# One transposition type and one matmul shape in a fused long-convolution and gated-MLP kernel

## The chip, the core and the metric

The kernel runs on one core of a Trainium2 chip. The metric is the device time of one execution in microseconds (us). Before the change it is 233.99 us, the median of three runs (233.98 to 234.03). In what follows PE is TensorE, PEld its weight loads, DVE VectorE, ACT ScalarE, POOL GpSimd, and SP the engine whose queue issues nearly all DMAs.

## What is computed

The input x has 2048 rows of 640 elements; xn is its layer norm. The output is x plus two branches of xn.

```python
k_shift = sum over t of k_pad[:, t:t + S, :] * shift_k[:, ks - 1 - t]   # 4 taps
kv  = k_shift * v
y   = irfft(rfft(kv_pad) * rfft(kf_pad))[:S]       # long convolution, length 2048, per channel, with ssm_k
y   = y + kv * ssm_D
A   = q * y                                        # q = xn
B   = (sigmoid(xn @ w_gate) * (xn @ w_up)) @ w_down    # 640 -> 1728 -> 640
out = x + A + B
```

The kernel adds ssm_D to the first sample of the filter h (ssm_k), so that the term kv * ssm_D comes out of the convolution itself.

## The kernel before

**Branch B** goes over the rows in four rounds t of 512. For each of 13 blocks fc of 128 hidden features there is a gate product (`gate_mm`, five matmuls of 512 columns), a sigmoid on ACT (`gate_ev`), an up product (`up_mm`, five more) and a multiplication on DVE that writes hT (`up_ev`, L286). A fourteenth half block has its own functions. Then `down_mm` (L315) turns hT into the output rows and `down_ev` (L320, DVE) adds them to x. The products, the down products and the last stage of the convolution all take their PSUM tiles from one ring of four banks, psG. A tile of that ring can be written again only when its reader is through: for an up product that is `up_ev`, for a down product `down_ev`, both on DVE.

**Branch A** goes over the 640 channels in five chunks c of 128. A chunk's time samples are held as (p, b): time = 16 p + b, with p on the 128 partitions and b in 0 to 15. One tile per chunk, kvh, has shape [128, 2, 16, 128]: plane 0 is kv, plane 1 is the filter h; there are two such tiles in turn.

- `kv_op` (L348 to L357, 16 DVE instructions a chunk) makes kv in plane 0, in two halves of eight b.
- h comes from DRAM as [channel, time] into the tile hn and has to be turned so that time lies on partitions. `h_turn(c, n)` (L334) does that on DVE with the engine's 32 x 32 block transposition, two instructions a chunk, each for half of the b. It reads hn as 4-byte elements, that is pairs of neighbouring samples, so each instruction moves 512 elements a partition, and the result holds the two samples of a pair next to each other: h of sample b = 2 b' + e and channel c lies at (b', c, e).
- `add_D` (L328, POOL) adds ssm_D to one row of the turned h.
- `st1_mm(c, n)` is the first stage of the transform. For each of four b it multiplies the table S1 (128 x 128 weights) with kv's 128 columns (L374) and with h's 128 columns (L376), which it reads with a step of two elements. Both results go side by side into one PSUM tile of the ring psC (two tiles), which `st1_ev` copies out, mostly on ACT. The eight calls of a chunk hold 64 matmuls, 320 in all.
- Further stages follow: a trip through DRAM, `st2_mm` (L418), the product of the two spectra on DVE (`prod`, L431 and L433), the inverse `inv1_mm` (L447), another trip through DRAM, `inv2_mm` (L488), and `inv2_q` and `inv2_x` on DVE, which multiply by xn and add to x.

**The order** of all this is written out by hand: each engine's instructions are issued in the order of one string of letters (`ORDER`), H being `h_turn`, a `st1_mm`, k one instruction of `kv_op`, u the DVE side of branch B, g the PE side. An engine takes its instructions strictly in that order, so an instruction that takes longer delays everything behind it on that engine.

Of the kernel before, what the change touches and what calls it, by code (L numbers as in the profile page):

```python
# [11 lines left out]
F32 = mybir.dt.float32  # L12
# [7 lines left out]
P = 128  # L20
NB = S // P
# [36 lines left out]
def kernel(  # L58
# [14 lines left out]
    nc = tc.nc  # L73
# [27 lines left out]
    S1 = S1t.bitcast(BF16)  # L101
# [23 lines left out]
    cin = [dict() for _ in range(NC)]  # L125
# [36 lines left out]
    def slot(c):  # L162

        if "kvh" not in cin[c]:
            cin[c]["kvh"] = cv.tile([P, 2, NB, P], BF16, name="kvh", bufs=2)
        return cin[c]["kvh"]
# [157 lines left out]


    def add_D(c):
        h0 = cin[c]["kvh"][0:1, 1, 0:2, :].rearrange("p b c -> p (b c)").rearrange("p (c e) -> p e c", e=2)[:, 0, :]
        nc.gpsimd.tensor_tensor(h0, h0, cin[c]["dr"][:, :], ALU.add)  # L328

    def h_turn(c, n):  # L330

        hv = cin[c]["hn"].bitcast(F32).rearrange("p k (r b) -> p b k r", b=8)
        to = slot(c)[:, 1, :, :].rearrange("p b c -> p (b c)").bitcast(F32).rearrange("p (b k r) -> p b k r", b=8, k=4)
        nc.vector.transpose(to[:, 4 * n:4 * n + 4, :, :], hv[:, 4 * n:4 * n + 4, :, :])  # L334

    def kv_op(c, n):

# [28 lines left out]
    def st1_mm(c, n):  # L366

        h, n4 = divmod(n, 4)
        if n == 0:
            chunks[c]["d1"] = dr.tile([P, 2, NB, 2 * P], BF16, name="d1", bufs=2)  # L370
        pss[n] = ps = psC.tile([P, 4, 2 * P], F32, name="ps1", tag="c")
        for i in range(4):
            b = 4 * n4 + i
            nc.tensor.matmul(ps[:, i, 0:P], lhsT=S1[:, b, h, :], rhs=cin[c]["kvh"][:, 0, b, :], start=True, stop=True)  # L374
            hp = cin[c]["kvh"][:, 1, :, :].rearrange("p b c -> p (b c)").rearrange("p (b c e) -> p b e c", b=8, e=2)
            nc.tensor.matmul(ps[:, i, P:2 * P], lhsT=S1[:, b, h, :], rhs=hp[:, b // 2, b % 2, :], start=True, stop=True)  # L376

    def st1_ev(c, n, copy=act_copy):
        d = chunks[c]
# [222 lines left out]
    for c in range(NC):  # L602
        for n in range(2):
            step("H", h_turn, c, n)
        step("D", add_D, c)
        for n in range(8):
            step("a", st1_mm, c, n)
            step("A", st1_ev, c, n)
# [101 lines left out]
```

## Time and profile before

| what | value |
|---|---|
| median of three runs | 233.99 us |
| span of the profiled execution, first to last instruction | 232.4 us |
| what lies around the span (median minus span) | 1.6 us |
| PEld busy | 130.7 us, 2201 loads |
| ACT busy | 123.0 us, 154 instructions |
| POOL busy | 13.3 us, 26 instructions |
| h_turn starts, ten instructions | from 30.9 us to 120.4 us |
| st1_mm starts | from 41.4 us to 162.8 us |
| granted PE clock, mean over the span | 1.000 |

The page of a profile gives busy times; matmuls are pipelined, so the busy time of a group of them (its instructions' union) is more than what it adds to the chain. What a matmul adds is the distance between the starts of neighbours. In the trace, L374 is followed by L376 after 55.2 ns in the mean (160 pairs), L376 by the next L374 after 58.5 ns (129 pairs without other work between); a matmul of 320 columns by its like after 136 ns, one of 512 columns after 216 ns.

### The profile page before, as it was taken

The numbers are of one execution on the slowest core, as the hardware profiler recorded it, in microseconds if no ns is written. First come the engines' busy times: TensorE is split into PE (matmuls) and PEld (weight loads), VectorE is DVE, ScalarE is ACT, GpSimd is POOL, SyncE is SP. The second block draws the span as 40 slices with busy tenths as digits, with TensorE's granted clock in tenths as the row PEclk, the third lists the DMA queues.
The fourth block names the chain that finished last, engine by engine and source line by source line (L and its number), as shares of the span: only waits on it lengthen the run. The fifth ranks groups of instructions, "written<-read, shape, count | busy, mean of one in ns | idle before, by whom it ended". The sixth has DMA issues, their size and how long they took to land.

```text
span 232.4 us, 5436 instructions
## 1 busy us (share of the span) xinstructions
PE 227.3 (98%) x2201; PEld 130.7 (56%) x2201; DVE 203.9 (88%) x362; ACT 123.0 (53%) x154; POOL 13.3 (6%) x26
## 2 busy tenths in 40 slices
PE   7999999999999999999999999999999999999995
PEld 2754445877454556667554544478654544446772
DVE  5534799999989999999999999997799999997773
ACT  2433232595354877766775847673555667752000
POOL 5210010040001100000010300000000000000000
PEclk9999999999999999999999999999999999999999
DMA  6999999799999979999989999597989998364784
GB/s 179 320 328 238 265 312 293 201 249 148 336 209 322 290 263 241 273 210 237 331 236 268 272 258 300 171 218 203 260 247 276 290 257 246 119 170 115 224 265 136
DMA packets 96303, 56.79 MB, mean 244 GB/s; under 512 B 55894, under 2 KB 90518, under 8 KB 96022
## 3 DMA queue, kind: packets, MB, share of 16 engines
q1 hardware_dynamic: 95846, 56.12, 90.6%
q8 instruction: 17, 0.28, 0.5%
q10 hardware_dynamic: 432, 0.33, 0.5%
q14 instruction: 8, 0.07, 0.1%
HBM read 36.12 MB, written 18.35 MB: 234 GB/s over the span
## 4 chain that ended last, share of the span: by engine, by line
PE 95%; DVE 2%; DMA 1%; ACT 0%; issue 0%
PE pd L315 27%; PE pu L271 24%; PE pg L271 24%; PE psb L488 4%; PE ps L376 4%; PE ps L374 4%; PE ps L418 3%; PE psa L447 2%; PE pg L292 2%; DVE st L198 1%; DMA x<-in_A_q_dram 1%; PE pu L262 1%; PE pg L262 1%; PE pt L244 0%; DVE xn L219 0%; ACT xnT L247 0%
## 5 line engine op out<-in xcount | busy, mean ns | idle before, releaser
L271 PEld LDWEIGHTS <-w 128*128 128x128 bf16 x500 | 46.6, 98 | 54.2 <-issue 4.7
L315 PE MATMUL pd<-wd,hT 128*128 128x320 bf16 (+2 forms) x448 | 66.0, 299 | 0.0
L271 PE MATMUL pg<-xnT,w 128*128 128x512 bf16 x250 | 62.2, 379 | 0.1
L271 PE MATMUL pu<-xnT,w 128*128 128x512 bf16 x250 | 62.2, 379 | 0.0
L315 PEld LDWEIGHTS <-hT 128*128 128x128 bf16 x448 | 41.7, 98 | 18.2 <-issue 2.4
L280 ACT ACTIVATE sig<-pg 128x512 bf16<-128x512 f32 x52 | 31.1, 601 | 31.1 <-PE pg L271 27.3
L286 DVE TENSOR_TENSOR hT<-sig,pu 128x512 bf16<-128x512 bf16 x52 | 34.9, 680 | 11.6 <-PE pu L271 7.5
L234 ACT CAST xz<-ps 128x1024 bf16<-128x1024 f32 x36 | 35.1, 1014 | 15.8 <-PE ps L418 15.7
L234 ACT CAST t<-ps 128x1024 bf16<-128x1024 f32 x24 | 23.7, 1013 | 16.3 <-PE ps L376 14.1
L433 DVE TENSOR_TENSOR xz<-xz 128x2048 bf16<-128x2048 bf16 x20 | 24.4, 1219 | 0.2
L376 PE MATMUL ps<-kvh,S1t 128*128 128x128 bf16 x160 | 21.4, 219 | 0.0
L374 PE MATMUL ps<-kvh,S1t 128*128 128x128 bf16 x160 | 21.4, 217 | 0.0
L354 DVE TENSOR_TENSOR acc<-acc,tmp 128x1024 bf16<-128x1024 bf16 x30 | 20.4, 681 | 0.3
L352 DVE TENSOR_TENSOR tmp<-kx,sc 128x1024 bf16<-128x1024 bf16 x30 | 20.4, 680 | 0.3
L320 DVE TENSOR_TENSOR x<-pd,x 128x320 bf16<-128x320 f32 (+2 forms) x32 | 15.2, 482 | 3.8 <-PE pd L315 3.6
L374 PEld LDWEIGHTS <-S1t 128*128 128x128 bf16 x160 | 15.5, 97 | 2.5
L376 PEld LDWEIGHTS <-S1t 128*128 128x128 bf16 x160 | 15.4, 96 | 2.5
L234 ACT CAST TBt<-ps 128x1024 bf16<-128x1024 f32 x14 | 13.8, 1012 | 4.0 <-PE ps L376 3.9
L198 DVE BATCH_NORM_STATS2 st<-x 128x6 f32<-128x320 bf16 x32 | 13.9, 475 | 1.9 <-DMA x<-in_A_q_dram 1.9
L493 DVE TENSOR_TENSOR yx<-psb,xn 128x512 bf16<-128x512 f32 x20 | 13.7, 686 | 1.4 <-PE psb L488 0.8
L431 DVE STREAM_SHUFFLE xz<-xz 128x512 f32<-128x512 f32 x20 | 14.6, 728 | 0.0
L234 ACT CAST ao<-psa 128x1024 bf16<-128x1024 f32 x9 | 9.0, 1013 | 8.3 <-PE psa L447 6.9
(55 smaller groups left out, 159.8 us busy)
## 6 DMA issues: line engine op xcount, KB each, us to landing
t<-d SPq DMA_DIRECT2D x15, 512.0 KB, 6.0
d<-t SPq DMA_DIRECT2D x13, 512.0 KB, 4.9
d<-TBt SPq DMA_DIRECT2D x7, 512.0 KB, 5.8
d<-ao SPq DMA_DIRECT2D x6, 512.0 KB, 5.5
bi<-d SPq DMA_DIRECT2D x6, 512.0 KB, 5.3
kx<-in_A_k_dram SPq DMA_DIRECT2D x10, 256.0 KB, 5.9
hn<-in_A_ssm_k_dram SPq DMA_DIRECT2D x20, 128.0 KB, 5.0
kvh<-in_A_v_dram SPq DMA_DIRECT2D x10, 256.0 KB, 5.2
```

Source lines behind the costliest of these rows:

```text
L198: nc.vector.bn_stats(d["st"][:, i, s2, :], x[:, b, s2 * 320:(s2 + 1) * 320])
L234: nc.scalar.copy(out=out, in_=in_)
L271: nc.tensor.matmul(pg[:, :], lhsT=w[:, c, u * UP + fc * P:u * UP + (fc + 1) * P], rhs=xnT[:, :, c, :], start=(c == 0), stop=(c == NC - 1))
L280: nc.scalar.activation(sig[fc][:, :], pgs[0, fc][:, :], ACT.Sigmoid)
L286: nc.vector.tensor_tensor(hT[:, fc, :], sig[fc][:, :], pgs[1, fc][:, :], ALU.mult)
L315: nc.tensor.matmul(pd[:, :], lhsT=hT[:, fc, bb * P:(bb + 1) * P], rhs=wd[:, fc, es], start=(fc == 0), stop=(fc == NFC - 1))
L320: nc.vector.tensor_tensor(x[:, 4 * t + bb, es], pds[bb, half][:, :], x[:, 4 * t + bb, es], ALU.add)
L352: nc.vector.tensor_tensor(d["tmp"][:, :, :], kx[:, lo + 3 - m:hi + 3 - m, :], sb(m), ALU.mult)
L354: nc.vector.tensor_tensor(d["acc"][:, :, :], d["acc"][:, :, :], d["tmp"][:, :, :], ALU.add)
L374: nc.tensor.matmul(ps[:, i, 0:P], lhsT=S1[:, b, h, :], rhs=cin[c]["kvh"][:, 0, b, :], start=True, stop=True)
L376: nc.tensor.matmul(ps[:, i, P:2 * P], lhsT=S1[:, b, h, :], rhs=hp[:, b // 2, b % 2, :], start=True, stop=True)
L433: nc.vector.tensor_tensor(z[:, 1:3, :, :], z[:, 0:1, :, :].to_broadcast((P, 2, 8, P)), z[:, 1:3, :, :], ALU.mult)
```

## The change

The diff has two parts. `h_turn` reads hn as 2-byte elements and writes plane 1 in the same layout as plane 0, (b, channel); each of the ten instructions now moves 1024 elements a partition where it moved 512 of twice the size, and the bytes are the same. `add_D` follows the new layout. In `st1_mm` the two matmuls of 128 columns with the same weights become one of 256 columns that takes both planes, so that there are 160 in place of 320. The order string is the same.

```diff
     def add_D(c):
-        h0 = cin[c]["kvh"][0:1, 1, 0:2, :].rearrange("p b c -> p (b c)").rearrange("p (c e) -> p e c", e=2)[:, 0, :]
+        h0 = cin[c]["kvh"][0:1, 1, 0, :]
         nc.gpsimd.tensor_tensor(h0, h0, cin[c]["dr"][:, :], ALU.add)

     def h_turn(c, n):

-        hv = cin[c]["hn"].bitcast(F32).rearrange("p k (r b) -> p b k r", b=8)
-        to = slot(c)[:, 1, :, :].rearrange("p b c -> p (b c)").bitcast(F32).rearrange("p (b k r) -> p b k r", b=8, k=4)
-        nc.vector.transpose(to[:, 4 * n:4 * n + 4, :, :], hv[:, 4 * n:4 * n + 4, :, :])
+        hv = cin[c]["hn"].rearrange("p k (r b) -> p b k r", b=NB)
+        to = slot(c)[:, 1, :, :].rearrange("p b (k r) -> p b k r", k=4)
+        nc.vector.transpose(to[:, 8 * n:8 * n + 8, :, :], hv[:, 8 * n:8 * n + 8, :, :])
...
             b = 4 * n4 + i
-            nc.tensor.matmul(ps[:, i, 0:P], lhsT=S1[:, b, h, :], rhs=cin[c]["kvh"][:, 0, b, :], start=True, stop=True)
-            hp = cin[c]["kvh"][:, 1, :, :].rearrange("p b c -> p (b c)").rearrange("p (b c e) -> p b e c", b=8, e=2)
-            nc.tensor.matmul(ps[:, i, P:2 * P], lhsT=S1[:, b, h, :], rhs=hp[:, b // 2, b % 2, :], start=True, stop=True)
+            nc.tensor.matmul(ps[:, i, :], lhsT=S1[:, b, h, :], rhs=cin[c]["kvh"][:, :, b, :], start=True, stop=True)
```

## The prediction

> **What bounds the kernel now.** I read the page first: the busy times, the slices, and the chain that ended last.
>
> ```profile
> PE 227.3 (98%) x2201; PEld 130.7 (56%) x2201; DVE 203.9 (88%) x362; ACT 123.0 (53%) x154; POOL 13.3 (6%) x26
> ...
> DVE  5534799999989999999999999997799999997773
> ...
> PEclk9999999999999999999999999999999999999999
> ...
> PE 95%; DVE 2%; DMA 1%; ACT 0%; issue 0%
> ```
>
> PE carries the chain. But DVE is at 9 tenths in nearly every slice from the seventh on, so the second view is the window in which the ten transpositions and nearly all of the first stage lie.
>
> ```profile
> 30.30:158.40 128.10, 128.02 (x1199) 74.97 (x1197) 124.15 (x221) 80.68 (x99) 7.99 (x10) 1.00 0.96 255
> ```
>
> After the stretch and its length come PE, PEld, DVE, ACT and POOL busy. PE is busy for 128.0 of 128.1 us and DVE for 124.2 (the rest is mostly gaps of some 0.03 us between dependent instructions). Two engines are full at once; the chain names one. What tells whether DVE has room is its own timeline: in this stretch it waits over 0.2 us for others three times, the last at the very end.
>
> ```profile
> 65.18 0.69 DVE L286 TENSOR_TENSOR hT<-sig,pu 128x512 bf16<-128x512 bf16 x1 [0.46 <-ACT sig L280]
> 68.83 0.69 DVE L286 TENSOR_TENSOR hT<-sig,pu 128x512 bf16<-128x512 bf16 x1 [0.26 <-ACT sig L280]
> 158.43 1.23 DVE L237 CAST t<-ps 128x1024 bf16<-128x1024 f32 x1 [1.22 <-PE ps L376]
> ```
>
> The fourth view is the groups of instructions:
>
> ```profile
> L376 PE MATMUL ps<-kvh,S1t 128*128 128x128 bf16 x160 | 21.4, 219 | 0.0
> L374 PE MATMUL ps<-kvh,S1t 128*128 128x128 bf16 x160 | 21.4, 217 | 0.0
> L354 DVE TENSOR_TENSOR acc<-acc,tmp 128x1024 bf16<-128x1024 bf16 x30 | 20.4, 681 | 0.3
> L431 DVE STREAM_SHUFFLE xz<-xz 128x512 f32<-128x512 f32 x20 | 14.6, 728 | 0.0
> L334 DVE STREAM_TRANSPOSE kvh<-hn 128x512 f32<-128x512 f32 x10 | 10.9, 1098 | 0.0
> ```
>
> A transposition takes 1098 ns for 512 elements, a shuffle of 512 contiguous elements of the same size 728.
>
> **PE's part.** A pair L374, L376 now takes 55.2 + 58.5 = 113.7 ns from start to start. Between 320 columns (136 ns) and 512 (216 ns) a column costs 80 / 192 = 0.417 ns; 256 columns come to 136 - 64 x 0.417 = 109.3. So 160 pairs save 160 x 4.4 = 0.7 us, 0.14 us a chunk. Bounds: the jump between the two planes could cost what the step of two costs now, 3.3 ns (saving 0.2 us), or nothing. The 160 weight loads that fall away lay beside matmuls (PEld 56% busy): nothing. `add_D` (POOL, 0.4 to 0.8 us, 6% busy) is the same instruction on contiguous elements: nothing.
>
> **DVE's part.** No 2-byte transposition stands in this trace. From below: 2-byte multiplications such as L354 move 1024 elements in the time in which L286 moves 512 with one 4-byte operand (start to start of the next independent instruction 0.60 us each); if a transposition did that it would drop from 1.03 to about 0.6 us, 0.43 less. From above: twice the whole instruction, 1.03 us more. I take the row itself: same engine, same instruction, the same step of 32 bytes between the elements read (8 of 4 bytes before, 16 of 2 bytes after). It takes 1.027 us from its start to the next one's in the mean of the nine that stand alone or end a pair. About 0.08 of that is fixed: measured the same way, L433 takes 1.13 for 2048 elements and L352 0.60 for 1024, which leaves 0.07; the copy L237 takes 1.13 for 1024 and the shuffle 0.62 for 512, which leaves 0.11. So an element costs 0.947 / 512 = 1.85 ns, against 0.54 / 512 = 1.05 in the shuffle. I hold that this is the price of an element that is fetched alone, and that it does not halve with the element's size. Then a new instruction takes 1024 x 1.85 + 80 = 1.97 us, 0.95 more; ten of them 9.5 us. Within this theory the added 512 elements cost at least the shuffle's rate, 0.54 us, and at most 1.03.
>
> [...]
>
> **From DVE's delay to the end.** DVE issues in order, so each transposition delays all behind it. I follow DVE's lag D against the old times and ask at each place where PE needs DVE how far ahead DVE was (the slack: PE's old start minus DVE's old end). The tightest are in the ring psG, where an up product needs the bank that `up_ev` of two blocks before frees. The last of them that counts:
>
> ```profile
> 121.44 0.63 DVE L286 TENSOR_TENSOR hT<-sig,pu 128x512 bf16<-128x512 bf16 x1
> ...
> 122.45 0.59 PE L271 MATMUL pu<-xnT,w 128*128 128x512 bf16 x2
> ```
>
> DVE ends at 122.07, PE starts at 122.45: slack 0.38.
>
> - Two transpositions from 30.9: D = 1.9. The up product at 35.41 had no slack (`up_ev` ended at 35.57 by the records): PE is 1.9 late.
> - Third, 42.3: D = 2.85. At 54.50 the first stage starts 0.07 after kv of chunk 1 is done: PE 2.8 late.
> - Fourth, 55.7: D = 3.8; slack 0.48 at 63.39: PE 3.3 late. DVE's waits of 0.46 and 0.26 take D down to PE's 3.3.
> - Fifth and sixth, 71.6 and 81.9: D = 5.2; slack 0.36 at 89.99: PE 4.9 late.
> - Seventh and eighth, 95.2: D = 7.1; slack 0.82 at 116.78: 6.3.
> - Ninth and tenth, 118.8: D = 9.0; slack 0.38 at 122.45: **PE 8.6 late**.
>
> Behind this PE is full and nothing gives the time back: DVE's later waits (1.22 us at 158.43 and others) are waits for PE, which is late itself. PE's own saving mostly goes under, since PE waits for DVE until 122; only the pairs after it count, 32 of chunk 4, 0.14 us. The sum is +8.6 - 0.1 = +8.5 us. The span goes from 232.4 to 240.9, and with the 1.6 us around it the median from 234.0 to **242.5 us**. In general the sum is ten times the added price less about 1.0: 0.54 gives 238.4, 1.03 gives 243.3. If DVE had had cover for the lag (it has none before 158), only the part over it would show.
>
> SP's queue waits behind hn's loads for `h_turn` (the load of the next chunk needs hn free), and wr1, rd2 and the rest stand behind them. That delay is D, and PE is late by nearly as much, so I add nothing; if a transfer becomes the last to arrive it is by D - PE's delay, under 0.9 us, in the middle, and the next step of D covers it. Bound 0 to 0.9.
>
> **Rivals.**
>
> 1. *The transposition goes by bytes* (place: L334; price: none; it decides if 2-byte elements take half a 4-byte element's time). [...] Against it: nothing in the 1.85 ns hints at bytes, and the shuffle, which moves 4 bytes an element, costs 1.05. Then DVE stays as it is and PE may gain only what the slacks allow: 0.38 at 122.45, then 0.14 on chunk 4: 234.0 - 0.5 = 233.5 us. Not slower.
> 2. *One element a cycle, hops or none.* Priced at the shuffle's 1.05 ns, 1024 elements and 0.08 come to 1.15 us, 0.12 more; by the same walk D is 1.2 less 0.2 for the waits, PE 0.6 late, 234.6 us. Against it: the 4-byte instruction doesn't run at that rate. [...]
> 3. *Two elements a cycle*, 0.6 us: DVE gains room, PE keeps all of its 0.7 us: 233.3. Nothing but L354 speaks for it.
> 4. *DVE's lag is partly covered*, because PE's order lets slack grow that I don't see: some 4 us in place of 8.5, 238. Against it: slacks under 0.5 us at 35.4, 54.5, 63.4, 90.0 and 122.5.
> [...]
>
> **Chances.** Forecast 0.80; rivals 0.05, 0.05, 0.03, 0.04, 0.03. The range reaches from the lower price of the theory, 238.4, with rival 4 nearly in it, to its upper price with the queue's 0.9: 243.3 + 0.9 = 244.2, rounded to 244.4. What lies outside is rivals 1, 2, 3 and 5, 0.16, and a little of the forecast's own tails. A measurement of this kernel can tell 0.2%, 0.5 us, from no change. Faster by more: rival 3 and half of rival 1, 0.06. Within: half of rival 1 and half of rival 2, 0.05. Slower: 0.89.
>
> **What would show it.** Price: L334 at about 2.0 us (start to next start), ten times. Path: DVE at 98% or more between 30 and 165, and PE with about 8.5 us of idle time, named as waits for DVE's hT, kvh or x (L286, L357, L320) or for ACT's sig behind them; the chain of waits should move from PE to DVE in this stretch. PE's part: one L374 group of 160, 109 ns apart. The forecast is wrong if L334 stays near 1.1 us, or if it doubles and PE still shows no idle time.

## The result and the profile after

The changed kernel takes 242.44 us (median of six runs, 242.32 to 244.08) against 234.07 (233.98 to 234.36) for the kernel before on the same chip. The ratio is 1.037, with a 95% interval of 1.0343 to 1.0397. The profiled execution has a span of 240.6 us where it had 232.4.

The page of the changed kernel: busy times, DVE's slices, and the chain that ended last.

```profile
PE 227.9 (95%) x2041; PEld 127.9 (53%) x2041; DVE 212.8 (88%) x362; ACT 123.2 (51%) x154; POOL 13.3 (6%) x26
...
DVE  5544899999999999999999999997889999898673
...
PE 62%; DVE 27%; issue 6%; DMA 3%; ACT 1%; SPq 0%; DVEq 0%
```

PE has 160 instructions less and about the same busy time, DVE has 8.9 us more in the same 362 instructions. The chain, which was PE's to 95%, now runs over DVE for 27% of the span. DVE's share of the span is 88% as before: the span grew with it, so the share shows nothing. The stretch that ran from 30.3 to 158.4 us now ends at about 167:

```profile
30.30:167.00 136.70, 129.36 (x1056) 72.87 (x1055) 133.38 (x222) 80.93 (x99) 7.97 (x10) 1.00 0.92 238
```

After the stretch and its length, PE's busy time comes first, DVE's third. Before, both filled 128.1 us (128.0 and 124.2); now DVE fills 133.4 of 136.7 and PE leaves 7.3 idle. The groups that the change touches (busy time, mean ns of one, idle time before them and what ended it):

```profile
L374 PE MATMUL ps<-kvh,S1t 128*128 128x256 bf16 x160 | 22.7, 273 | 2.5 <-DVE kvh L357 2.5
...
L334 DVE STREAM_TRANSPOSE kvh<-hn 128x1024 bf16<-128x1024 bf16 x10 | 20.2, 2024 | 0.0
```

A transposition went from 1098 to 2024 ns; from its start to the next instruction's, which is what DVE loses, from 1.025 to 1.947 us (mean of ten each; the prediction has 1.027). The 273 ns of a matmul are no cost, since matmuls overlap: a merged one starts 109.3 ns after the one before (mean of 128 places without other work between). Where PE waits is seen in its timeline: these six rows are all its waits over 0.1 us behind 30 us, with what ended each in brackets.

```profile
37.50 1.24 PE L292 MATMUL pg<-xnT,w 128*128 128x512 bf16 x5 [0.82 <-DVE hT L286]
...
57.38 0.60 PE L374 MATMUL ps<-kvh,S1t 128*128 128x256 bf16 x4 [1.74 <-DVE kvh L357]
...
66.11 0.61 PE L374 MATMUL ps<-kvh,S1t 128*128 128x256 bf16 x4 [0.40 <-DVE kvh L357]
...
91.63 0.61 PE L374 MATMUL ps<-kvh,S1t 128*128 128x256 bf16 x4 [0.40 <-DVE kvh L357]
...
116.68 0.43 PE L416 MATMUL ps<-t,SMt 32*32 32x512 bf16 x14 [1.72 <-DVE t L237]
...
130.77 1.24 PE L271 MATMUL pu<-xnT,w 128*128 128x512 bf16 x5 [2.16 <-DVE hT L286]
```

All six end with DVE, and none comes after 131 us; before the change there was none. Five of them wait for what the prediction's walk follows, hT or kv; the one at 116.68 waits for a tile of the ring psC, which DVE's copy L237 has to read first. They add up to 7.2 us. A wait is counted from the modelled end of the matmul ahead, which lies some 0.16 us behind the time at which the next could have started (a product of 512 columns lasts 379 ns and its like follows after 216), so six waits stand for about 8.2 us. That is the difference of the spans. Matched instruction by instruction with the kernel before, PE is 0.03 us late at 33 us, 1.1 at 41, 2.9 at 54.5, 3.2 at 63, 3.6 at 90, 6.0 at 117, 8.3 at 122.5 (old times), and 8.2 at the end.

### The profile page after: what moved, and what is told of

Same layout as the page of the kernel before. It is cut to its first block, busy times and chain, and to the rows that moved or that the text cites. A ratio compares the mean times of both kernels' runs of the same rounds, so it can differ in the third digit from the quotient of the medians.

```text
span 240.6 us, 5118 instructions
## 1 busy us (share of the span) xinstructions
PE 227.9 (95%) x2041; PEld 127.9 (53%) x2041; DVE 212.8 (88%) x362; ACT 123.2 (51%) x154; POOL 13.3 (6%) x26
## 4 chain that ended last, share of the span: by engine, by line
PE 62%; DVE 27%; issue 6%; DMA 3%; ACT 1%; SPq 0%; DVEq 0%
PE pd L315 16%; PE pu L271 16%; PE pg L271 15%; DVE acc L354 5%; DVE kvh L334 5%; PE psb L486 4%; DVE tmp L352 4%; DVE st L198 3%; PE ps L374 3%; PE ps L416 3%; PE psa L445 2%; DVE hT L286 2%; DVE x L320 2%; DMA kx<-in_A_k_dram 2%; DVE kvh L357 2%
## 5 line engine op out<-in xcount | busy, mean ns | idle before, releaser
L271 PEld LDWEIGHTS <-w 128*128 128x128 bf16 x500 | 47.3, 98 | 56.8 <-issue 6.9
L315 PEld LDWEIGHTS <-hT 128*128 128x128 bf16 x448 | 42.2, 98 | 18.9 <-issue 2.6
L374 PE MATMUL ps<-kvh,S1t 128*128 128x256 bf16 x160 | 22.7, 273 | 2.5 <-DVE kvh L357 2.5
L354 DVE TENSOR_TENSOR acc<-acc,tmp 128x1024 bf16<-128x1024 bf16 x30 | 20.4, 682 | 0.3
L374 PEld LDWEIGHTS <-S1t 128*128 128x128 bf16 x160 | 15.3, 98 | 9.7 <-DVE kvh L357 2.1
L334 DVE STREAM_TRANSPOSE kvh<-hn 128x1024 bf16<-128x1024 bf16 x10 | 20.2, 2024 | 0.0
L486 PEld LDWEIGHTS <-TBt 128*128 128x128 bf16 x160 | 10.0, 98 | 3.5 <-issue 1.8
## 6 DMA issues: line engine op xcount, KB each, us to landing
hn<-in_A_ssm_k_dram SPq DMA_DIRECT2D x20, 128.0 KB, 3.7
```

The source lines that it names most:

```text
L271: nc.tensor.matmul(pg[:, :], lhsT=w[:, c, u * UP + fc * P:u * UP + (fc + 1) * P], rhs=xnT[:, :, c, :], start=(c == 0), stop=(c == NC - 1))
L315: nc.tensor.matmul(pd[:, :], lhsT=hT[:, fc, bb * P:(bb + 1) * P], rhs=wd[:, fc, es], start=(fc == 0), stop=(fc == NFC - 1))
L334: nc.vector.transpose(to[:, 8 * n:8 * n + 8, :, :], hv[:, 8 * n:8 * n + 8, :, :])
L354: nc.vector.tensor_tensor(d["acc"][:, :, :], d["acc"][:, :, :], d["tmp"][:, :, :], ALU.add)
L374: nc.tensor.matmul(ps[:, i, :], lhsT=S1[:, b, h, :], rhs=cin[c]["kvh"][:, :, b, :], start=True, stop=True)
```

## The experiments

The kernels below ran on chips on which single executions spread more than in the comparison above: the kernel before took 234.4 to 234.5 us in the median, with 233.9 to 236.7 in all. So 0.4 us of a time that was expected against 234.0 is the chip's. Differences under about 0.5 us are therefore read from the traces, not from the medians.

### Is it the transposition or the matmul?

First each part of the change by itself. The transposition alone (an edit of the changed kernel):

```diff
-            nc.tensor.matmul(ps[:, i, :], lhsT=S1[:, b, h, :], rhs=cin[c]["kvh"][:, :, b, :], start=True, stop=True)
+            for s in range(2):
+                nc.tensor.matmul(ps[:, i, s * P:(s + 1) * P], lhsT=S1[:, b, h, :], rhs=cin[c]["kvh"][:, s, b, :], start=True, stop=True)
```

> The transposition alone: 2-byte elements and the new layout, but the first stage keeps two matmuls of 128 columns for each b (both on contiguous columns). Theory (DVE's price sets the end; PE's saving counts only behind the last place where PE waits for DVE): L334 at 1.95 us from start to start as in the changed kernel, the time within 0.3 us of the changed kernel's 242.4, that is 242.3 to 242.7. Rival (the merged matmul itself delays something): under 241.5. Rival (the merged matmul saves its full 0.7 us in the changed kernel): 243.1.

Measured: 242.64 us (242.38 to 242.87), ratio to the kernel before 1.034 (1.0293 to 1.0381). The transposition alone has the whole cost, and each instruction its new length:

```profile
L334 DVE STREAM_TRANSPOSE kvh<-hn 128x1024 bf16<-128x1024 bf16 x10 | 20.2, 2027 | 0.0
```

Its two contiguous matmuls of 128 columns start 56 ns apart, 112 ns a pair, so the pair of the old kernel (113.7) lost 1.7 ns to h's step of two elements, and the merge itself is worth 2.7 ns more.

The merge alone, on the kernel before:

```diff
-            nc.tensor.matmul(ps[:, i, 0:P], lhsT=S1[:, b, h, :], rhs=cin[c]["kvh"][:, 0, b, :], start=True, stop=True)
-            hp = cin[c]["kvh"][:, 1, :, :].rearrange("p b c -> p (b c)").rearrange("p (b c e) -> p b e c", b=8, e=2)
-            nc.tensor.matmul(ps[:, i, P:2 * P], lhsT=S1[:, b, h, :], rhs=hp[:, b // 2, b % 2, :], start=True, stop=True)
+            nc.tensor.matmul(ps[:, i, :], lhsT=S1[:, b, h, :], rhs=cin[c]["kvh"][:, :, b, :], start=True, stop=True)
```

> The matmul of 256 columns alone: the transposition stays at 4-byte elements, so that h's columns of two neighbouring samples are mixed in what is multiplied, and the output is not the reference's. Theory: one matmul each 109 ns in place of a pair in 113.7, but PE may run ahead of DVE only by the slacks: 234.0 - 0.5 = 233.5, and no longer than 234.1. Rival (matmul of two runs of 128 columns costs more than the pair): over 234.3. Rival (PE alone sets the time): the full 0.7 less, 233.3.

Measured: ratio 1.0023 (0.9992 to 1.0053), lowest run 233.52 against 233.87 before. The interval holds no change and the expected 0.5 us less is just outside it; the run excludes that the merge costs what the change costs, and can't settle its sign. One more kernel asked for that: the merge together with a cheaper transposition (contiguous reading, next section), so that DVE has room.

> The merged matmul with the 4-byte transposition read contiguously (0.63 us in place of 1.03, as measured in the contiguous run): what the merge is worth when DVE has room. Two samples of h are mixed in what is multiplied and samples land in wrong places, so the output is not the reference's. Theory (PE's saving is lost only because PE waits for DVE): the 0.7 us appear, 0.7 us under the kernel before (0.5 to 0.8). Rival (the merge saves nothing on PE, whatever DVE does): within 0.2 us of the kernel before.

Measured: ratio 1.0018 (0.9996 to 1.004), lowest 233.59 against 233.94 before. By the time the expected gain did not appear. The trace of one run, matched with the kernel before, shows where it went in that run: PE starts 0.62 us late (at 7 us, ahead of any changed instruction, behind x's first loads), loses 0.63 at 54.5, since DVE had waited 0.9 us for x, and 0.1 at 58 behind a DMA of xnT. From there its lag only shrinks, from 1.24 us to 0.76, by about 0.018 with every call of `st1_mm`; with the 0.12 of the first chunk that makes 0.6 of the 0.7 us. In the 2-byte run of the next section, where DVE has room too, PE's lag shrinks in the same way, by 0.34 us between 58 and 122. So the traces have the saving on PE, and landings of DMAs outweigh it in this one. That they do so in the median of all runs is not shown, and neither is a gain in time.

### Why does a 2-byte transposition cost twice?

The forecast rested on a price, 1.85 ns, for an element that is read with a step of 32 bytes. The test changes only the order in which hn is read:

```diff
-        hv = cin[c]["hn"].rearrange("p k (r b) -> p b k r", b=NB)
+        hv = cin[c]["hn"].rearrange("p k (b r) -> p b k r", b=NB)
```

> The changed kernel with one thing altered: the transposition reads hn in contiguous order (32 neighbouring samples a block) in place of every sixteenth sample. The bytes, the count of elements and all other work are the same; the samples of h land in the wrong places, so the output is not the reference's. Theory (1.85 ns is the price of an element fetched alone with a step of 32 bytes): L334 falls to about 1.15 us from start to start (1024 x 1.05 + 80 ns), and the time to 234.6 (234.1 to 235.2). Rival (the transposition takes near two cycles an element however it reads): L334 stays at 1.95 us and the time at 242.4.

The same in the kernel before, on 4-byte elements:

> The kernel before with the transposition of 4-byte elements reading contiguously, output not the reference's for the same reason. Theory: L334 falls from 1.03 to 0.62 us from start to start, ten times 0.41 off DVE; PE has no idle time to give, so the time stays within 0.2 us of 234.0. Rival (two cycles an element however it reads): L334 at 1.03 and 234.0.

The transposition's group in the first and in the second of these runs:

```profile
L334 DVE STREAM_TRANSPOSE kvh<-hn 128x1024 bf16<-128x1024 bf16 x10 | 12.2, 1231 | 0.0
```

```profile
L334 DVE STREAM_TRANSPOSE kvh<-hn 128x512 f32<-128x512 f32 x10 | 6.9, 699 | 0.0
```

2024 became 1231 ns and 1098 became 699; to the next start 1.16 and 0.62 us. The 512 elements between the two contiguous runs cost 532 ns, 1.04 each. The 2-byte run took 235.47 us (234.91 to 236.31), ratio 1.0036 (1.0011 to 1.0062), so 7 us of the change's cost went away with the order of reading alone, at the same number of elements and bytes. In the trace PE ends 0.7 us late, 0.2 of it from ahead of the first transposition. The expected 234.6 is 1.0026 times 234.0 and lies within the interval; the 235.47 itself lies above the expected 235.2, as this chip's kernel before lies above 234.0. The 4-byte run took 234.34, ratio 0.9992 (0.9968 to 1.0015): ten times 0.4 us off DVE bought nothing, as PE had no idle time to give.

How far apart must elements lie? One kernel gave each chunk another step, on 2-byte elements, and one on 4-byte elements. The edit of the first (the second reads 4-byte elements with steps of 8, 4, 2, 1 and 16 elements):

```diff
-        hv = cin[c]["hn"].rearrange("p k (r b) -> p b k r", b=NB)
-        to = slot(c)[:, 1, :, :].rearrange("p b (k r) -> p b k r", k=4)
-        nc.vector.transpose(to[:, 8 * n:8 * n + 8, :, :], hv[:, 8 * n:8 * n + 8, :, :])
+        step = (16, 8, 4, 2, 1)[c]
+        flat = cin[c]["hn"].rearrange("p k t -> p (k t)")[:, 1024 * n:1024 * n + 1024]
+        hv = flat.rearrange("p (a r b) -> p a b r", b=step, r=32)
+        to = slot(c)[:, 1, 8 * n:8 * n + 8, :].rearrange("p b c -> p (b c)").rearrange("p (a b r) -> p a b r", b=step, r=32)
+        nc.vector.transpose(to, hv)
```

> The price of the step, 2-byte elements: the changed kernel, with the transposition of chunk 0, 1, 2, 3, 4 reading every 16th, 8th, 4th, 2nd element and each element (steps of 32, 16, 8, 4 and 2 bytes), 1024 elements each time; h's samples land in wrong places, so the output is not the reference's. Theory (an element that is fetched alone costs 1.85 ns, neighbours 1.04): chunk 0 at 2.0 us an instruction, chunk 4 at 1.23, and the time between 234.6 and 242.4. [...] Rival (the price grows with the step): five different durations.

> The same with 4-byte elements: the kernel before, with chunk 0, 1, 2, 3, 4 reading with steps of 32, 16, 8, 4 and 64 bytes, 512 elements each time; the output is not the reference's for the same reason. [...] The time stays within 0.5 us of the kernel before.

DVE's timeline in the first, one row for the steps of 32, 16, 8 and 2 bytes (start, length):

```profile
31.01 2.03 DVE L336 STREAM_TRANSPOSE kvh<-hn 128x1024 bf16<-128x1024 bf16 x1
...
44.30 2.02 DVE L336 STREAM_TRANSPOSE kvh<-hn 128x1024 bf16<-128x1024 bf16 x1
...
74.85 1.24 DVE L336 STREAM_TRANSPOSE kvh<-hn 128x1024 bf16<-128x1024 bf16 x1
...
122.54 1.24 DVE L336 STREAM_TRANSPOSE kvh<-hn 128x1024 bf16<-128x1024 bf16 x1
```

And in the second, for 32, 16, 8 and 64 bytes:

```profile
30.93 1.10 DVE L337 STREAM_TRANSPOSE kvh<-hn 128x512 f32<-128x512 f32 x1
...
57.70 1.09 DVE L337 STREAM_TRANSPOSE kvh<-hn 128x512 f32<-128x512 f32 x1
...
73.34 0.70 DVE L337 STREAM_TRANSPOSE kvh<-hn 128x512 f32<-128x512 f32 x1
...
120.42 1.05 DVE L337 STREAM_TRANSPOSE kvh<-hn 128x512 f32<-128x512 f32 x1
```

There are two prices and no steady slope: steps of 2, 4 and 8 bytes cost 1.24 us for 1024 elements, steps of 16 and 32 cost 2.0; with 4-byte elements 0.70 for 512 at 4 and 8 bytes, 1.1 at 16 and 32, and a little less, 1.05, at 64. In both runs the edge lies between the steps of 8 and 16 bytes. The times, one run each, are 237.7 and 235.96 us beside 235.17 for the kernel before on that chip. The second is 0.8 us over, where at most 0.5 was expected; in its trace DVE waits 1.28 us for hn and 0.42 for x ahead of 46 us, and PE is 1.7 us late from 57 us to the end, so its time says nothing about the price. The durations of the transpositions do.

### Does the lag add up as the walk said?

The change in the last two chunks only, and in the first three only (`c >= 3` or `c <= 2` selects old or new code in `add_D`, `h_turn` and `st1_mm`):

> A partial dose: chunks 0 to 2 as before the change, chunks 3 and 4 as after it (four of the ten transpositions in 2-byte elements, at 95 and 119 us, and their first stage merged). Theory (lag adds up and is passed to PE at the next place without slack): D = 4 x 0.92 = 3.7 by 121, slack 0.4 at 122.45, 0.1 saved on PE: 234.0 + 3.2 = 237.2 (236.7 to 237.8). Rival (the early chunks, where PE has least slack, make the cost, the late ones are covered): under 235.5. Rival (a share of the whole, 4 / 10 of 8.4): 237.4, which this run can't tell from the theory; the first three chunks alone can.

> The other part of the dose: chunks 0 to 2 as after the change, 3 and 4 as before it. Theory: D = 6 x 0.92 - 0.5 (DVE's two waits) = 5.0 by 83, and nothing is added later, so that the places with slack 0.8 at 116.8 and 0.4 at 122.45 decide: 234.0 + 5.0 - 0.4 - 0.1 = 238.5 (238.0 to 239.1). The two partial doses then add up to some 0.7 less than the whole, since each has the slack once. Rival (share of the whole, 6 / 10 of 8.4): 239.0. Rival (the late chunks make the cost): under 236.5.

Measured: 237.94 us (237.67 to 240.23), ratio 1.0159 (1.011 to 1.0207), and 239.46 (238.83 to 240.92), ratio 1.0208 (1.0156 to 1.026). Both lie above the middle of what was expected, by 0.7 and 1.0 us, and just outside the expected ranges, which ended at 237.8 and 239.1; 0.4 us of each is the chip's. Early and late chunks both count: the rival of the covered late chunks is out, and so is the one of the covered early ones. The rival of plain shares (237.4 and 239.0) is not: with the chip's 0.4 us it fits these times better than the theory, and the two doses together cost no less than the whole, where 0.7 us less was expected.

The traces, matched with the kernel before at its own times, split the excess. In the late dose PE is 0.5 us late at 59, before any changed instruction (DVE had waited 0.52 us for x), and 3.8 to 3.9 us late behind 122: 3.3 from the dose, where 3.2 was expected. In the early dose PE is 0.64 late from the start, and DVE's lag is 5.6 us from 83 to 127. PE is 5.25 late behind 122, so 4.6 came from DVE, where 4.5 was expected. It is 5.7 late from 143 on, and that last step is no wait for DVE: the product of the last convolution stage at 149.11 in this run (143.41 before) waits 0.28 us for the DMA that reads bi, which SP issued at 142.07 where it had issued it at 134.61. So the queue's term, bounded by 0 to 0.9 us in the prediction, is real: 0.4 us where no later lag of DVE covers it. The walk along DVE is good to 0.1 us in these two runs; landings of DMAs, which are not in its sum, make the rest.

### Two tries at a version that beats both

If DVE gets a contiguous transposition of 4-byte elements and PE the merged matmul, both gain. That needs another pair: two channels in place of two samples, laid side by side and sorted by sample ahead of the transposition. POOL was to do it (an edit of the changed kernel):

```diff
     def h_turn(c, n):

-        hv = cin[c]["hn"].rearrange("p k (r b) -> p b k r", b=NB)
-        to = slot(c)[:, 1, :, :].rearrange("p b (k r) -> p b k r", k=4)
-        nc.vector.transpose(to[:, 8 * n:8 * n + 8, :, :], hv[:, 8 * n:8 * n + 8, :, :])
+        h1 = slot(c)[:, 1, :, :]
+        pairs = h1.rearrange("p b (k r e) -> p b k r e", k=2, e=2)
+        bs = slice(8 * n, 8 * n + 8)
+        for kk in range(2):
+            src = cin[c]["hn"][:, 2 * kk:2 * kk + 2, :].rearrange("p e (r b) -> p b r e", b=NB)
+            nc.gpsimd.tensor_copy(pairs[:, bs, kk, :, :], src[:, bs, :, :])
+        hv = h1.rearrange("p b c -> p (b c)").bitcast(F32).rearrange("p (b k r) -> p b k r", b=NB, k=2)
+        nc.vector.transpose(hv[:, bs, :, :], hv[:, bs, :, :])
```

The loads of hn (in `load_h`, not shown) change with it.

> A version that keeps the merged matmul and gives DVE a cheaper transposition than before the change. hn is loaded with channels 64 kk + 2 r + e on partition r (twice as many DMAs, each half as large); POOL copies it so that the two channels of a pair and then 32 samples of a block lie next to each other; DVE turns 512 elements of 4 bytes read contiguously. The pair that stays together is now a pair of channels, so h comes out in kv's layout. Theory: L334 at 0.63 us from start to start as in the contiguous run, ten times 0.40 off DVE, so DVE no longer holds PE back and PE keeps its 0.7 us: 233.3 (233.1 to 233.8). Rivals: POOL's copies (some 1.2 us each, 2 a transposition) come too late for DVE, or slow DVE while they run: over 234.5; SP's queue is held up by the added loads: over 234.5.

Measured: 246.67 us, ratio 1.0495 (1.0452 to 1.0538). All that the rivals name shows in the trace; how the 12 us divide among them was not measured. SP is busier with the loads: it issues chunk 1's eight from 35.9 to 42.6 us, where the changed kernel issues its four from 36.3 to 38.3. The copies, 1.22 us each, wait for hn, and DVE waits 7.1 us in all for them. And DVE's instructions beside the copies stretch; in this window of the timeline L361, L364 and L355 are what L354, L357 and L348 were, and take 1.55, 0.94 and 1.48 us in place of 0.65 to 0.80:

```profile
29.51 5.18 POOL L339 COPY kvh<-hn 128x512 bf16<-128x512 bf16 x4 [14.55 <-DMA hn<-in_A_ssm_k_dram]
29.61 1.55 DVE L361 TENSOR_TENSOR acc<-acc,tmp 128x1024 bf16<-128x1024 bf16 x1
...
32.16 0.71 DVE L341 STREAM_TRANSPOSE kvh<-kvh 128x512 f32<-128x512 f32 x1 [0.40 <-POOL kvh L339]
...
32.80 0.94 DVE L364 TENSOR_TENSOR kvh<-acc,kvh 128x1024 bf16<-128x1024 bf16 x1
...
33.77 1.48 DVE L355 TENSOR_TENSOR acc<-kx,sc 128x1024 bf16<-128x1024 bf16 x1
```

So the copies moved to ACT (`nc.scalar.copy`), at places of the order where ACT had gaps, the second chunk's first transposition went behind two layer norm steps, and hn's loads were four again:

> The version with pairs of channels, with two things altered against the one that copied on POOL: ACT makes the copies (20 of 512 elements, each put where ACT had a gap of 1 to 3 us), since POOL's copies came late and the DVE instructions beside them took up to twice as long; and hn is loaded with four DMAs a chunk in place of eight. Theory: ACT's copies take 0.65 us each, 13 us in all where ACT is 53% busy, DVE's instructions keep their length, L334's successor takes 0.63 us, and PE keeps the merge's saving: 0.5 to 0.7 us under the kernel before. Rival (ACT's copies delay sigmoids and evacuations that PE waits for, or read with a step and cost 1 us or more each): over the kernel before by 0.5 us or more.

Measured: 251.72 us, ratio 1.0716 (1.069 to 1.0741). The transposition took its 703 ns, and the rest went wrong:

```profile
L337 ACT COPY kvh<-hn 128x512 bf16<-128x512 bf16 x20 | 21.5, 1119 | 9.8 <-DMA hn<-in_A_ssm_k_dram 9.8
...
L344 DVE STREAM_TRANSPOSE kvh<-kvh 128x512 f32<-128x512 f32 x10 | 7.0, 703 | 8.5 <-ACT kvh L337 8.5
```

The copies read with a step and cost 1.12 us, not 0.65, and stand in ACT's order, so that ACT waited 9.8 us for hn with sigmoids and evacuations behind it, and DVE 8.5 us for ACT. A part of the time of both versions may be PE's clock: in the profiled executions the mean granted over the span was 0.985 and 0.986, in the kernel before 1.000. As an estimate, 1.5% of 245.8 us and 1.4% of 250.1, that is at most 3.7 us of the 12 and 3.5 of the 17. No version here beats the kernel before, and PE has at most 0.7 us to give.

## Why the prediction was right, and where it was off

- **Both engines full, DVE with no cover.** Right: all of PE's new waits end with DVE, and PE's lag of 8.2 us stays to the end. DVE is busy for 97.6% of 30 to 167 us, where 98% was named as the sign.
- **The price.** Forecast 0.95 us more a transposition, measured 0.92: an added element cost 1.80 ns, not 1.85. That the price lies in how far apart the elements are read, and does not halve with their size, is shown by the contiguous runs: the fixed part and 1.04 ns an element remain (1.16 us for 1024 of 2 bytes, 0.62 for 512 of 4), and the rest is the step. How DVE fetches an element, alone or with its neighbours, no run shows; what they show is two prices, with the edge between steps of 8 and 16 bytes. Rivals 1 to 3 fall with the measured 1.95 us, and rival 4 with the lag of 8.2 us. The fifth chance, 0.03, stood for a 2-byte element that costs more than a 4-byte one; no trace had spoken for it, and 1.80 against 1.85 ns excludes it. Rival 2's price was the contiguous run's (1.15 us forecast, 1.16 measured). L354, which the prediction calls a multiplication, is an addition; the time that is read from it stands.
- **PE's saving.** 109.3 ns forecast and measured for a merged matmul; 0.13 us behind 122 us kept (8.31 to 8.18), 0.14 forecast.
- **The walk.** The sum of +8.5 was 8.2; with the measured price its rule (ten times the price less 1.0) gives 8.2. The median came still nearer to the forecast, to 0.1 us, and that is luck: the span was 0.3 us under its forecast, and a little more than 1.6 us lay around it. DVE's own lag went as walked, 1.9, 2.8, 3.7, 5.0, 6.8 and 8.6 us where the walk has 1.9, 2.85, 3.8, 5.2, 7.1 and 9.0.
- **Where PE waits.** PE's steps between were worse: 1.9 us late at 35.4 was 1.0 at 36.5, and 4.9 at 90 was 3.6. In both the place that I named did not bind. The product at 35.44 ran while DVE had not yet begun the `up_ev` that I took for its release (36.78); the wait came one product later, when that `up_ev` ended. The old trace had said so: there the product starts at 35.41, ahead of the end of that `up_ev` at 35.57, so it can't have waited for it. So a bank is not always freed by the reader that a plain count of four back names, and the slacks taken that way were too small there. Since a lag that is not passed on stays in DVE, the next place with a true wait collected it (116.68 and 130.77), and the sum hardly noticed. Of the six waits only those at 57.38 and 130.77 stand where the walk names a place. Those at 66.11 and 91.63 are the first stage's for kv, a little ahead of the up products that it names, and the one at 116.68 is in psC, a ring that it didn't ask about.
- **The queue's 0.9 us** was not needed: no wait of PE in the list ends with a DMA. In the kernel with the first three chunks changed such a wait came, and cost 0.4 us.

## What to carry to other kernels

Where two engines are full, price a change by what it does to the engine that the chain does not name, and ask at each place where one needs the other, in every ring that they share, how far ahead it was. Here the sum of lags less what the slacks and DVE's few waits took was the cost to 0.3 us, and what PE saved ahead of its last wait was lost. In these runs the price of DVE's transposition went by elements and by where they lie, not by bytes: with a step of 32 bytes the same bytes took 2.02 us as 1024 elements of 2 bytes and 1.10 as 512 of 4, and elements read with steps of 16, 32 or 64 bytes cost 0.7 to 0.8 ns each on top of 1.04. Before giving work to an idle engine, look at what it reads, what stands behind it in its order, and what it does to the engine beside it.

## What the runs showed of the hardware that was not expected

- Among steps of 2 to 32 bytes for 2-byte elements, and of 4 to 64 for 4-byte elements, the price of DVE's transposition showed one edge, between 8 and 16 bytes (1.24 and 2.0 us for 1024, 0.70 and 1.05 to 1.1 for 512).
- While POOL copied between SBUF tiles, from 29.5 to 34.7 us, three of DVE's instructions with two inputs from SBUF took 1.55, 0.94 and 1.48 us where they take 0.65 to 0.80 in the contiguous runs. The transposition in that window took 0.71, against 0.70 with no copy beside it, and the multiplication that reads one input from PSUM (L288) 0.68.
- ACT's copy of 512 2-byte elements took 1.12 us when it gathered pairs from far apart, against 0.66 for the copy of 512 elements with a step of four (`taps`, L151).
